# One list of 2833 steps replaced by another, in packed attention with a SwiGLU MLP

## The chip, the cores and the metric

The kernel runs on one core of one Trainium2 chip. The metric is the device time of one execution in microseconds (us). A trace of one profiled execution shows what each engine did: PE (TensorE, the matmuls), DVE (VectorE), ACT (ScalarE), POOL (GpSimd) and SP (SyncE, which here issues the transfers).

## The reference

```python
def _attn_ref(q, k, v, p):            # q, k, v: 8 x 8 x 576 x 64; p: 8 x 8 x 32 x 64
    scale = 1.0 / np.sqrt(q.shape[-1])
    def sm_attn(qq, kk, vv):
        s = scale * np.matmul(qq, kk.transpose(0, 1, 3, 2))
        s = s - np.max(s, axis=-1, keepdims=True)
        a = np.exp(s)
        a = a / (np.sum(a, axis=-1, keepdims=True) + 1e-09)
        return np.matmul(a, vv)
    p_packed = sm_attn(p, k, v)
    return sm_attn(q, p_packed, p_packed)

def _moe_ref(x, w_gate, w_val, w_out, rms_g):   # x: 4608 x 512; w: 512 x 1536 (twice), 1536 x 512
    rms = np.sqrt(np.mean(x * x, axis=-1, keepdims=True) + 1e-06)
    xn = x / rms * rms_g
    g = xn @ w_gate
    silu = g * (1.0 / (1.0 + np.exp(-g)))
    return silu * (xn @ w_val) @ w_out
```

The 8 heads' attention outputs, 64 wide each, stand side by side as the 512 features of a token. The three weight matrices arrive in double precision, as pairs of 32-bit words.

## The kernel before, in words

Attention over 32 packed keys per head comes first, then the norm and the MLP. Stage 1 lets the 32 packed vectors of a batch attend to its 576 keys (scores L747 and L756, softmax L778, values L887). The 4608 tokens are cut into 12 units of 384; units 1, 4, 7 and 10 span two batches, so their attention has twice as many small matmuls. For a unit: scores of the queries against the packed keys (L1231, L1238), softmax (L1252 to L1262 on DVE, L1257 on ACT), attention values (L1309, L1318), norm and transposition into aTu, the MLP's input (L1136 on ACT and L1138 on DVE for unit 0, a transposing transfer issued at L1396 later), 24 blocks of gate and value matmuls (L1439), SiLU and products (L1520, L1523, L1542, L1545), output matmuls (L1506), store (L1577, L1580).

In the first 60 us or so the weights are fetched and turned into single precision on the chip: ACT (L387, L396), POOL (L391) and DVE (L393, L398, L401, L403) share the pieces, PE sums their squares (L447, L454), packed weights are formed for the first batches (L1040), and each piece is split into a high half (L352, ACT) and a low half (L354, DVE), kept in `ring`, which L1439 reads. Stage 1 of a later batch goes through a_0x and a_1x: exponentials are split into 16-bit halves, transposed by a transfer (L856), added up on POOL (L861), and only then used by PE (L887).

All this is written as some 90 coroutines ("chains", among them keys, stage 1, queries, attention, packed weights, one for each weight piece, the MLP, the stores). `Plan.run` walks the table ORDER: each pair of base-64 digits is a chain's number, and that chain issues its next step on that step's engine. So ORDER alone sets the order within each engine's stream. Buffers (four PSUM banks pm_0x to pm_3x, the halves psa and psb, six large buffers big_0x to big_5x, two each of aTu, o and others) go to the steps in the same order, so a table also decides which buffer a step has and whose release it waits for. FILLS lists at which PE steps how many filler matmuls are put in: L1603, 128x256 on constants, whose result nobody reads.

Of the kernel before, what the change touches and what calls it, by code (L numbers as in the profile page):

```python
# [44 lines left out]
class Plan:  # L45
# [89 lines left out]
    "ATAwAYAyArAvAYAxAWATAsAWAvAyAXAZAPAxArAsArArArAYArATAZAsAYATArAzAZAsAZATAyAzAZAyAaA0AoAsA0AsATAsAaAzArAaA0ATAsAT"
    "AzA1A1A1AsA1AoAcAsA0ATAcA2ArAdACATACATA3AsACAdARAcA3A2AfA2A3AdATAfA3A2ARACATAeA4A4ACATA4ATATAeAQAQA5ARATATACA5AC"
    "ATATAeARATACATATATATARATACAQACAgAfACARAgAQARACATASARACAhAQARAQAhAQARACA4AAAAAAAAAAAAARASA5ARAgAAARAQATARARARAQA6"
    "ATATATATARAhATATARA5ARASAQATATARARAAATATATA6ATARARAAA6AAA6A7ARATATARAQASAAAAARA8ATAAA9ARARAAAAAAATA8ATATATATA9AT"
    "ARATATAAATAAATARA9A-ARA9ARATATA+AABAA+BAATATASA+AABAA+ARASAABBAABABCBBATATBDAABCASARASAABCBBBDBCATATARBEBBBEBDBE"
    "BFBEBDATAAATATBFAAASARBGBFAABGBFASAAATBGBIBGATBHBHBHBHBIARAAATATASARBKBIARATARBKASBIBLBKBKARACBMBLARATATACBMBMBM"  # L140
    "ARBLBNBLBNARACACACACATATATATBOATBJAQBNATBNATATATATATACAQBOAQACARARAQARARARARARBPAQBPBOARACBPACBPACACBJAAAAARAAAC"
    "ACAQACBOACACATA-ATATATATATATATATAAAAACAAAAATAAAQATAAATATATATATACATACAQAQAAAAAQAAACATACAAACACAABQATA7ATACACAQBRBR"
    "ACATATATATACAAACACASBQAAAAASATACAbAbBSAAARBSASBSACAbAABSARATATASATATATBTBTATBTARBTBVATATARBVAbAABWBUBWATATATATBV"
    "BWBVBXASAABXAAASAABXBWBYBXARBZATBYACAbBZATARBYBaBaATATATAbBZAABYBaBbBZATAABbASAbBbBaBcACASAABcATATARBbARAABdBeAb"
    "AbAABeBdBcBdBdATATAbATARARASAbBcARBfATBeAbARARBeAbARBfBgBfATAbATBUAAACBgACARAbBgBfBhATATBgBjAbBjATATATATBhAbACAR"
    "ATATATARASACACBhBjACARARBiAQAQATAbACBhAbATARBkAbAQBkBjATATARATATACBkARARARARARBkACAQBlASACACACACAbACATATAQARBiAC"
    "ACACAAACAbATATATATATAAATACAQAQAbATATATATATATAQAbAQAAAQAABlAQAQATAAAAACAAACAAASAbAbBmACACAbAAACACBnBnAAACATACATAT"
    "ACATAAATACACACBnAbACBmATAABnAbASBoBoBoARBoARACATATBpAABpASAbATATAABqARBqBrATATARBqBsACAbBqBrBsATATATARAAAbBsBrBs"
    "BrAbATBtBtAbARACBuBtAABuBtAAATATBvAbACATATAABvATATBuBvAbARAABuBwBvAABwBxAABwAbBxARAABxAbATBwARARATATARARAbByATAT"
    "BxARARAAByBzAbByAAARByATAbBzARATBzB0ARB0ATAbB0BzARARAAAAB0ATB1ATAbATB1ARB2AAB1AQB1AQAQAAB2AAARAbB2ARAQB2ATATAbAT"  # L150
    "ATARATATATATATAQATAQAQARAQATATAQAbAQARACATATAbARAQAbATATAbB4ACAbARAbATATATATATATAbATATACARARARAbACAbATATATATB4AT"
    "ATAbACATATATACAbB3B5AbACAbARARAbARAbACAbACACARACAbACB3B5AAAAAAAAATACAbATATATAAAAATB6AAAbACB7ATATB8ACARARB7ASAbB7"
    "AbB8ATB8B7B-AbB8B9B9B9B9AbATATATACB-ACARB+AbAAB-AAAAB+B-ASATB+CBCACACAB+AbCAATATCBAbARATATARARCCCCASCBAbARARACCB"
    "AAACCDCDAAAbARB6CCCEATCEATACCECDCECDAAACCCCFAAASCFATCFARARCFATCGCGCGACACCHATAACGAAACARATCHACARACARCIATCHAAATACCH"
    "ARARCIACACARCJARARATARAAATATAQACAAATCIARATAQCIATACCJCKACAAAAATATAQCJCJASAACLCKAQACARCKCKAQAAATATATATATCLACATATAQ"
    "CLAQAQATATATATATATATAQAQAAATATCLAQASAAAAAAAACMATATCOARCNACATATATARATARATATAACOCNACCNARATATARCPACCNACARACATATATAT"
    "ATATARCQCRATATCSCRCRCSACCRATATASCSARACACCTCUCTCUCUCTATATACCSCTACARCVCUARARATATCVASARCVCWCVARATARCXCWATACCXCYARCY"
    "CXCWACACACCYCWCXACASCZCZCZATATATAACaCZAAAACMACCYCaARATATATCbCaCbATARATCaCbCcACARACCcAACbCPACCdCcATCdATCcATATAQCQ"
    "AAAAAAARAQARACCeAQCdAACdAACeATCfATAQAAACATATATATARAAAACfARARATASACAQAACfCeACARARAQCgATCfACAQATAAAQATCeACCgAQARAA"
    "AQACACACATACATATATAAATATATAQATATATACATATACChCgACCgACACASAAAQAACiATATATATATAACiAACjARCiAAAAARCiAAARASATATATATCkAC"  # L160
    "ATATATATATATCjCkAACkATARAACkARClCmATATATCnAACmATATCnAACmAACnCnARCoCmCoATATCpCoCoATCqACCpACARAACpCqCqCpATATATCrAC"
    "CqACCrARACATATATCrCtCrCtACARATACATCtCuCuARACARCtCvARCuACCvARCvATATARCuATCwCvCwATATATAQClCxARAQAQARCsACACARCxCwAQ"
    "CwAQARAQAQCyCxATATATATCyATCyATACACACACCxATATCyARChARAAACATARARAQARAQATATAAACARATATATATATATATATAAARATATAAAAATATAT"
    "ATAQARARATATATATAAARAQAAAAARAAARATCzACAAAAAAAAARC0CsACACARATATATAAAAATATATACATATACCzC1AAAAARC2ARC2ATAAATATATC3C2"
    "C3ASC2C4C3C4ACC4C3ATATARC5ACAAC5C5C6C5C6ACC6ACASATACC7ARC6ATC7ACC7AAC8C7ACC8ATATATATC4ACC8C9AAACC9ACC8AAC-AAARAC"
    "C9ASC9C+C+C-ACC+ARC+ARATATDAACATC-DAAAC-ASATARDADCDAATACDBDBDBAAARDBARATDCDDAADCATATAADDAADDDCDEATARARATATDDATAT"
    "ATATAQDFARATACDEAQDFARC0DFARASACATATACARAQARARDEAADFATDHDEATATATARDGAQDGDHDGARARAQDIAQASACARAQARDJDGARATATATAQDJ"
    "ATATATATATATATATDHATAQACDHDHATACDJAQATATATATDIATATATDKDHDHARAQARATATATATATACDKDHDJARDHARACDLATATATDMDNARDMATATDN"
    "DMACDMACASDODNDPDODPDODPDPDNATATDOATATDQDQDRDQDHATATDRDQDSDRDHASDTDSDRDTATATATDTDTDUDSATATDSDUACARDVDVDUASDHDUAT"
    "DWACARDXACDXDWDXACDXDVACATATATDVDYDWDYDYATATDZDHDYDZATDaAQC1AQDHACDaATATARATATDLDZASARAQACATATAQACARARDaATARARDZ"  # L170
    "AQACARARDaDWAQARAQATATATATATDcATACATATAQAQDbACARAQAQARATATARARACARDbATATARAQACARDcARATARATACACACATACATATATATARAT"
    "ATATARACACACACACDbDdARACASATDeDdATDbARDeARASATATDfATATDfACDeDfACDeDfARATATACDgATATATARDhDiARDhDiATDhDiDhATDjDjDj"
    "ATATATDiDjDkATATDkDlARDlACDkARATATATDlDlDmDmDkDmDnDmATATDoATARDoDnATDoDoDnARARDnATDpATATARDpDpDqDpARDqATATDqATAQ"
    "DrDqDrAQAQAQAQAQAQDrARDsAQDsATATATATATDrARAQDsATATATARARAQARDsARATATATATATARATATATATARAQDgATATATARARARARARATATAT"
# [1478 lines left out]
```

## Time and profile before

| | |
|---|---|
| median of 3 runs | 736.81 us (735.4 to 737.38) |
| profiled execution | 735.02 us, of which the span takes 732.8 us |
| granted clock of TensorE over the span | 0.998 of full speed |
| PE busy | 712.7 us, 97% of the span |
| DVE, ACT, POOL busy | 468.9, 476.0, 210.2 us |
| PE idle from 0 to 60 us | 8.7 us (60 less 51.31 busy) |
| last 13 us | PE busy 9.31 us |

The span runs from the first instruction to the last; the profiled time has some 2.2 us around it. PE is the engine that nearly fills the span, so the table is read by where PE has nothing to do, and why: in the first 60 us, in a few waits later, and at the end while the last tile is stored.

### The profile page before, as it was taken

Reading aid. Unit: us, or ns where it says so; the run is one execution under the profiler, and the core shown is the slowest. Engines: PE = TensorE matmul, PEld = TensorE weight load, DVE = VectorE, ACT = ScalarE, POOL = GpSimd, SP = SyncE. Lnnn points to the kernel's source line nnn. Section 1 sums busy time; section 2 is a strip of 40 time slices with the busy share of each in tenths; the row PEclk is TensorE's granted clock in tenths of the full one; section 3 lists DMA queues with packets and bytes.
Section 4 is the critical chain, followed back from the end, with each engine's and each line's share of the span. In section 5 each row is a group of like instructions: output and inputs, shape, how many; then the busy total and the mean of one; then the engine's idle time right before and its main releaser. Section 6 shows DMA issues by size and latency. Waiting matters only on the chain.

```text
span 732.8 us, 19527 instructions
## 1 busy us (share of the span) xinstructions
PE 712.7 (97%) x8164; PEld 432.1 (59%) x8164; DVE 468.9 (64%) x1032; ACT 476.0 (65%) x982; POOL 210.2 (29%) x228
## 2 busy tenths in 40 slices
...
GB/s 288 369 376 266 203 3 65 85 155 198 34 145 116 145 91 142 169 89 118 81 195 79 65 180 109 102 101 133 73 115 57 62 67 80 65 3 50 1 1 58
DMA packets 152922, 86.72 MB, mean 118 GB/s; under 512 B 116737, under 2 KB 140161, under 8 KB 152834
## 3 DMA queue, kind: packets, MB, share of 16 engines
...
q14 instruction: 24, 0.20, 0.1%
...
## 4 chain that ended last, share of the span: by engine, by line
PE 83%; DMA 6%; ACT 4%; DVE 3%; issue 2%; SPq 1%; POOL 0%; ACTq 0%; DVEq 0%; POOLq 0%
PE pm_3x L1439 10%; PE pm_2x L1506 10%; PE pm_1x L1439 9%; PE pm_2x L1439 9%; PE pm_0x L1439 9%; PE pm_0x L1506 7%; PE pm_1x L1506 7%; PE pm_3x L1506 6%; DMA ring<-in_moe_w_val_dram 2%; PE psa L1238 1%; DMA a_1x<-hl_0x 1%; PE psb L887 1%; DMA a_0x<-hl_0x 1%; PE pm_0x L1464 1%; PE pm_3x L1464 1%
## 5 line engine op out<-in xcount | busy, mean ns | idle before, releaser
L1439 PEld LDWEIGHTS <-ring 128*128 128x128 f16 x2304 | 204.4, 98 | 85.6 <-issue 13.2
L1506 PEld LDWEIGHTS <-hall 128*128 128x128 f16 x1188 | 113.5, 98 | 137.9 <-issue 8.5
L1545 POOL TENSOR_TENSOR hall<-t_1x,hall 128x384 f16<-128x384 f32 x67 | 64.3, 960 | 204.7 <-ACT hall L1542 196.1
L1545 POOL TENSOR_TENSOR hall<-t_0x,hall 128x384 f16<-128x384 f32 x61 | 58.6, 961 | 155.2 <-ACT hall L1542 150.4
L1506 PE MATMUL pm_2x<-wo,hall 128*128 128x512 f16 x360 | 81.2, 379 | 0.0
L1506 PE MATMUL pm_1x<-wo,hall 128*128 128x512 f16 x324 | 72.6, 379 | 0.6 <-ACT t_1x L1520 0.6
L1506 PE MATMUL pm_0x<-wo,hall 128*128 128x512 f16 x324 | 72.6, 379 | 0.0
L1439 PE MATMUL pm_3x<-aTu_1x,ring 128*128 128x384 f16 (+1 forms) x318 | 46.9, 290 | 0.1
L1439 PE MATMUL pm_3x<-aTu_0x,ring 128*128 128x192 f16 (+1 forms) x330 | 44.7, 280 | 0.0
L1439 PE MATMUL pm_2x<-aTu_1x,ring 128*128 128x192 f16 (+1 forms) x330 | 43.5, 276 | 0.5 <-DVE o_0x L1577 0.5
L1542 ACT CAST hall<-t_1x 128x384 f16<-128x384 f32 x69 | 34.9, 506 | 12.5 <-DVE t_1x L1523 12.3
L1542 ACT CAST hall<-t_0x 128x384 f16<-128x384 f32 x70 | 35.5, 507 | 11.6 <-DVE t_0x L1523 11.2
L1439 PE MATMUL pm_1x<-aTu_0x,ring 128*128 128x384 f16 (+1 forms) x288 | 42.4, 290 | 0.1
L1506 PE MATMUL pm_3x<-wo,hall 128*128 128x512 f16 x180 | 42.4, 389 | 0.0
L1439 PE MATMUL pm_0x<-aTu_0x,ring 128*128 128x384 f16 (+1 forms) x276 | 40.0, 288 | 0.0
L1439 PE MATMUL pm_1x<-aTu_1x,ring 128*128 128x384 f16 (+1 forms) x252 | 37.9, 292 | 0.9 <-issue 0.9
L1439 PE MATMUL pm_2x<-aTu_0x,ring 128*128 128x384 f16 (+1 forms) x258 | 37.8, 289 | 0.1
L1439 PE MATMUL pm_0x<-aTu_1x,ring 128*128 128x384 f16 (+1 forms) x252 | 36.6, 288 | 0.0
L1074 POOL TENSOR_TENSOR wgv<-o_0x,wgv 128x512 f16<-128x512 f32 x16 | 19.0, 1188 | 24.6 <-ACT wgv L1072 24.6
L1520 ACT ACT_TABLE_LOAD x15 | 19.2, 1283 | 10.4 <-PE pm_0x L1439 4.5
L861 POOL TENSOR_TENSOR a1T_0x<-a_1x 96x768 f32<-96x768 f16 x5 | 8.2, 1633 | 33.4 <-DMA a_1x<-hl_0x 33.4
L352 ACT ACTIVATE ring<-pm_0x 128x512 f16<-128x512 f32 x17 | 10.1, 592 | 7.7 <-PE pm_1x L1052 6.2
...
## 6 DMA issues: line engine op xcount, KB each, us to landing
...
```

Of the source, the lines that this page charges most:

```text
L352: nc.scalar.activation(hi, x, AF.Copy, scale=s)
L861: nc.gpsimd.tensor_tensor(a1T, x[:, 0], x[:, 1], ALU.add)
L887: nc.tensor.matmul(pp[32 * j : 32 * j + 32, :D], a1T[:, c, 32 * j : 32 * j + 32], vf[:, j, cv, :], start=(c == 0), stop=(c == NCK - 1),)
L1074: nc.gpsimd.tensor_tensor(wgv16[:, c, k, 1], st, wgv16[:, c, k, 0], ALU.subtract)
L1238: nc.tensor.matmul(ps2[o : o + n, i, :, pi, :], qT[:, lq, i, pi, o : o + n], packs[b][3][:, lp, pi, :, :], start=(j == 0), stop=(j == 2),)
L1439: nc.tensor.matmul(psi[:, :, o : o + n], pw[:, g, lw, w, f * P : (f + 1) * P], aT[:, :, la, g, o : o + n], start=(j == 0), stop=(j == 5),)
L1464: nc.tensor.matmul(pos[i], hall[:, ft, lh, i * P : (i + 1) * P], wo[:, ft, 1 - lw, :], start=(ft + n3 == 0), stop=(ft == NFT - 1 and n3 == 2),
L1506: nc.tensor.matmul(po, hall[:, ft, lh, ts], wo[:, ft, 1 - lw, :], start=(n == 0), stop=(n == 3 * NFT - 1))
L1520: nc.scalar.activation(t, pss[0][:, :UT], AF.Silu, scale=sc[:, c, 0:1])
L1542: nc.scalar.copy(hall[:, ft, 0, :], t)
L1545: nc.gpsimd.tensor_tensor(hall[:, ft, 1, :], t, hall[:, ft, 0, :], ALU.subtract)
```

## The change

The strings of ORDER and the tuple FILLS are replaced by others. Both lists have 2833 steps, the same steps of the same chains; no instruction's form changes. FILLS goes from 110 filler matmuls to 99. Ahead of the first gate matmul (L1439) there are 98 fillers where there were 110, and 21 transpositions of keys on PE (L628) where there were 27; the other six stand behind it.

```diff
 ORDER = (
-    "AEAEAAAAAAAAADAAAAAAAEAAADAAAAAAAAAAAAAAAAAAAEADAAAAAAAQAFABABAGAHAIAJAiAQAiAiAjAQAiAjAQAiAiAFAFAiAiADAiAjADAQAj"
...
+    "AEAAAAADAEAAAAAAAAAAAAADAAAAAAAAAAAAAAAAAAADAAAAAAAiAjAEAiAjAQAQAiAiADAiAFAQABAFABAiAiAjAQAjADAEAiAiAjAjAjAQAjAG"
...
 FILLS = (
-    (0, 30, "pm", 0), (5, 4, "psc", 0), (8, 5, "pa", -1), (24, 11, "pm", 0), (25, 8, "pm", 2),
-    (27, 37, "pm", 0), (30, 13, "psc", 0), (42, 2, "psc", 0),
+    (0, 30, "pm", 0), (5, 4, "psc", 0), (8, 5, "pa", -1), (18, 4, "psc", 0), (23, 5, "psc", 0),
+    (25, 7, "pm", 0), (26, 8, "pm", 0), (28, 32, "pm", 0), (31, 3, "psc", 0), (54, 1, "psc", 0),
```

The first place is VectorE early in the weight conversion. `t24`, `e_0x` belong to the softmax of unit 0, `wo32_78` is a raw weight piece, `wgv_77` the converted one, `tiny_13x` the sum of squares of a piece. Before:

```order
L1254 TENSOR_TENSOR e_0x_108<-psa_100,t24_0x_244 128x768
L398 SCALAR_TENSOR_TENSOR wgv_77<-wgv_77,wo32_78 128x4x256
L452 TENSOR_REDUCE tiny_13x_153<-pm_1x_95 128x2
L1259 TENSOR_REDUCE t24_1x_245<-e_0x_108 128x24
L1260 TENSOR_SCALAR t24_2x_246<-t24_1x_245 128x24
L1261 RECIPROCAL t24_2x_246<-t24_2x_246 128x24
L1262 TENSOR_TENSOR e_0x_108<-e_0x_108,t24_2x_246 128x768
L398 SCALAR_TENSOR_TENSOR wgv_77<-wgv_77,wo32_78 128x4x256
```

After:

```order
L1254 TENSOR_TENSOR e_0x_108<-psa_100,t24_0x_244 128x768
L452 TENSOR_REDUCE tiny_13x_153<-pm_3x_97 128x2
L398 SCALAR_TENSOR_TENSOR wgv_77<-wgv_77,wo32_78 128x4x256
L340 TENSOR_SCALAR tiny_14x_154<-pm_3x_97 128x2
L344 TENSOR_SCALAR tiny_14x_154<-tiny_14x_154 128x2
L345 TENSOR_SCALAR gv_r_80<-tiny_14x_154 128x2
L460 TENSOR_SCALAR ratio_81<-tiny_14x_154,gv_r_80 128x1
L398 SCALAR_TENSOR_TENSOR wgv_77<-wgv_77,wo32_78 128x4x256
L1259 TENSOR_REDUCE t24_1x_245<-e_0x_108 128x24
L1260 TENSOR_SCALAR t24_2x_246<-t24_1x_245 128x24
L1261 RECIPROCAL t24_2x_246<-t24_2x_246 128x24
L1262 TENSOR_TENSOR e_0x_108<-e_0x_108,t24_2x_246 128x768
```

The softmax sums and the division (L1259 to L1262) move behind one conversion (L398), and a piece's sum of squares with the four small steps that form its scale (L452, L340 to L460) moves ahead of two. In PE's stream the first packed weights (L1040) stood right behind the 16 L447 matmuls of that piece; now eight fillers and the sum over partitions of the piece (L454) stand between.

The second place is VectorE at the end of that stage, where its half of aTu(0), the first MLP input, is written (L1138). Before:

```order
L1023 TENSOR_SCALAR pgh_0x_132<-pg_0x_128,ratio_81 128x128
L354 SCALAR_TENSOR_TENSOR ring_87<-pm_2x_96,gv_r_80,ring_87 128x512
L393 SCALAR_TENSOR_TENSOR wgv_77<-wgv_77,wo32_78 128x4x256 x2
L594 COPY pT_0x_122<-pm_2x_96 128x256
L354 SCALAR_TENSOR_TENSOR ring_87<-pm_1x_95,gv_r_80,ring_87 128x512
L1138 SCALAR_TENSOR_TENSOR aTu_0x_111<-psa_100,aTu_0x_111 128x3x256
L354 SCALAR_TENSOR_TENSOR ring_87<-pm_3x_97,gv_r_80,ring_87 128x512
```

After:

```order
L1023 TENSOR_SCALAR pgh_0x_132<-pg_0x_128,ratio_81 128x128
L393 SCALAR_TENSOR_TENSOR wgv_77<-wgv_77,wo32_78 128x4x256 x2
L1138 SCALAR_TENSOR_TENSOR aTu_0x_111<-psa_100,aTu_0x_111 128x3x256
L594 COPY pT_0x_122<-pm_2x_96 128x256
L354 SCALAR_TENSOR_TENSOR ring_87<-pm_1x_95,gv_r_80,ring_87 128x512
L354 SCALAR_TENSOR_TENSOR ring_87<-pm_0x_94,gv_r_80,ring_87 128x512
```

Two low halves of weight pieces (L354) and the copy of the packed vectors (L594) move from ahead of L1138 to behind it. On ACT, two high halves (L352) move from ahead of aTu(0)'s other part (L1136) to behind it, and one query copy (L1175) the other way.

The third place is SyncE's queue of transfers around the second transposition of stage 1 for batch 2 (L856 on `a1_1x`). Before:

```order
L573 DMA pf_0x_121<-in_p_dram 32x2x64 x2
L1396 DMA_TRANSPOSE aTu_0x_111<-hl_0x_109 128x12x128
L573 DMA pf_0x_121<-in_p_dram 32x2x64
L1580 DMA out_0_dram<-o_1x_116 128x512
L573 DMA pf_0x_121<-in_p_dram 32x2x64
L551 DMA big_3x_105<-in_k_dram 96x4x384
L856 DMA_TRANSPOSE a1_1x_118<-hl_0x_109 128x12x128
L551 DMA big_4x_106<-in_k_dram 96x4x384
```

After:

```order
L573 DMA pf_0x_121<-in_p_dram 32x2x64
L551 DMA big_3x_105<-in_v_dram 96x4x384
L573 DMA pf_0x_121<-in_p_dram 32x2x64 x3
L1396 DMA_TRANSPOSE aTu_0x_111<-hl_0x_109 128x12x128
L551 DMA big_4x_106<-in_k_dram 96x4x384
L856 DMA_TRANSPOSE a1_1x_118<-hl_0x_109 128x12x128
L551 DMA big_0x_102<-in_k_dram 96x4x384
```

A store (L1580) and two of the loads of packed vectors (L573) no longer stand between the transposition of aTu and this one; a load of keys (L551) still does, and another stands behind it. PE's stream between the scores of that half batch (L756) and the values that need the transposition (L887) holds 51 output matmuls L1506 in both kernels.

## Rows read from the trace of the kernel before

**Rows 1.** The page: the span's heading and the busy times.

```profile
span 732.8 us, 19527 instructions
...
PE 712.7 (97%) x8164; PEld 432.1 (59%) x8164; DVE 468.9 (64%) x1032; ACT 476.0 (65%) x982; POOL 210.2 (29%) x228
```

**Rows 2.** Busy time by stretch: us from the start, length, each engine's busy time (instructions), granted clock, DMA share, GB/s.

```profile
0.00:60.00 60.00, 51.31 (x749) 39.23 (x750) 44.72 (x98) 41.28 (x72) 18.95 (x38) 1.00 1.02 349
...
60.00:733.00 673.00, 661.43 (x7418) 392.88 (x7416) 424.15 (x934) 434.68 (x911) 191.23 (x191) 1.00 0.45 98
```

**Rows 3.** What PE waited for before 60 us: line and releaser, total us, times, longest.

```profile
PE pm_1x L1603 <- POOL misc L263: 1.7, 1, 1.7
PE psb L454 <- DVE tiny_19x L452: 1.5, 1, 1.5
```

**Rows 4.** What PE waited for from 60 us on, the three that cost most.

```profile
PE psb L887 <- POOL a1T_0x L861: 3.4, 2, 1.8
PE psa L1318 <- issue: 2.1, 1, 2.1
PE pm_1x L1439 <- issue: 0.9, 1, 0.9
```

**Rows 5.** PE in the first conversions: start, us, engine, line, operation.

```profile
30.55 0.40 PE L1040 MATMUL pm_3x<-wgv,pg_0x 64*32 64x256 f32 x1
...
31.57 4.21 PE L1603 MATMUL pm_0x<-misc,margin 128*128 128x256 bf16 x37
36.75 0.85 PE L1112 MATMUL psb<-ident,e_0x 128*128 128x128 f32 x6 [0.96 <-ACT ring L352]
```

**Rows 6.** VectorE from 31 to 37 us.

```profile
31.03 0.96 DVE L1254 TENSOR_TENSOR e_0x<-psa,t_0x 128x768 f32<-128x768 f32 x1
31.90 1.22 DVE L398 SCALAR_TENSOR_TENSOR wgv<-wgv,wo 128x1024 uint32<-128x1024 uint32 x1
33.03 0.68 DVE L452 TENSOR_REDUCE tiny_13x<-pm_1x 128x2 f32<-128x512 f32 x1
33.63 0.94 DVE L1259 TENSOR_REDUCE t_1x<-e_0x 128x24 f32<-128x768 f32 x1
...
35.16 1.44 DVE L1262 TENSOR_TENSOR e_0x<-e_0x,t_2x 128x768 f32<-128x768 f32 x1
```

**Rows 7.** ScalarE from 35 to 41 us.

```profile
35.95 0.70 ACT L352 ACTIVATE ring<-pm_3x,gv_r 128x512 f16<-128x512 f32 x1
...
39.94 0.58 ACT L1122 ACTIVATE aT_0x<-psb 128x512 f32<-128x512 f32 x1
```

**Rows 8.** VectorE's last instructions ahead of the first attention block aTu(0).

```profile
57.90 0.41 DVE L594 COPY pT_0x<-pm_2x 128x256 f32<-128x256 f32 x1
58.23 0.73 DVE L354 SCALAR_TENSOR_TENSOR ring<-pm_1x,gv_r,ring 128x512 f16<-128x512 f32 x1
58.89 0.94 DVE L1138 SCALAR_TENSOR_TENSOR aTu_0x<-psa,aTu_0x 128x768 f16<-128x768 f32 x1
```

**Rows 9.** PE around the first MLP matmuls.

```profile
60.00 0.49 PE L628 MATMUL pm_0x<-ident,big_1x 128*128 128x128 f32 x3
60.33 1.14 PE L1439 MATMUL pm_2x<-aTu_0x,ring 128*128 128x384 f16 x6
```

**Rows 10.** The chain that ended last, 150 to 185 us: start, us, what.

```profile
167.22 5.53 DMA a_1x<-hl_0x
...
176.82 5.42 PE pm_3x L1506 x18
```

**Rows 11.** The chain at 233 us, the same transposition of the next batch.

```profile
232.92 3.70 DMA a_1x<-hl_0x
```

**Rows 12.** The chain at 332 us, as many output matmuls.

```profile
331.81 3.88 PE pm_2x L1506 x18
```

**Rows 13.** Busy time by stretch, 176 to 182 us.

```profile
176.00:182.00 6.00, 6.00 (x26) 2.32 (x24) 2.96 (x11) 4.81 (x14) 0.00 (x0) 0.72 0.91 219
```

**Rows 14.** The chain at 435 us, inside the attention of unit 7.

```profile
434.89 2.14 issue
```

More of the change, by code (lines that the diff above doesn't have):

```diff
@@ L135 @@
[L135 to L174, printed above, removed]
@@ new lines @@
+    "AHAiAjAFAiAFAjAQACAjAQAGACACACACAHAHAFACAFACAGAFAIARAJAGACAFAKALASAIAIAHAHAJAJARAHAHASARAIAHAJAKARAkARASALAKAKAk"
+    "AMALAkALAkARANASAlAMARAJALAJAJAlAJARAlANANAQAQAHARARALAMAFALASAlARAMARALANASARARARASAmAOAPAUAmAAAAAAAQARAQAQAAAA"
+    "ANAQARASARAmANARAOAQAnANAmARAOAnAVAPAoAPARAQANALASARAOAPASARApAnAWAAAAAAAPApApAAApAUAUAUAAAoAPAJAVAVAnATATAtAVAT"
+    "AUAPATAuAtATAPAAAWAWAAAAAAAWAVAtAXATAAAuASAUAtAvATAWAuAYAXAAAuAvAVAAAAAAATAAAwAYAXAvAoAoArASAXAxAvAYArAwAqAZAxAT"
+    "ATAYAqAxAyArAyAwAxATATArAYArAZAyArAsAWAYANAsAZArAoArAXATArAyAwAZAXAsATArAPA0AsAZA0AoAzAZAaAzATAsA0ATAzA0AsAaAaA1"
@@ new lines @@
+    "AdAzA1A1AsATAsATATAdArAdAsA1ATAsA2AcA3A2AcACA2AeA2AsACATATACACA4A3ACAeACA3ARA4AcATACARACACACACATA3ATATAgATATA5AC"
+    "AeAQACARAQAQAfACAgAgATATA5ARASA5AAAQA5AAAAAAAhAAATATATAfATARATAQARARAQAQA4ARAfASARARATAQAAAhA6AQAQARA6ATARA6ATAR"
+    "ATARARARAAARAAAAA4ATATATATAhATARARARA6ATATASATARARAAASARAQA8AAAAA7ATARARA9AAA8AAARA9A8A8AAATATATATARARATATATAAAA"
+    "ARATAAATAAATATATATATARA-AAATATARA+ARAABAA+BAA+ASAAAAATBAA+A-ATASBBBBBABCBBARBCATATBDBBBCASARBCAABDARBDASBEBEBEAT"
+    "BEATBFATATAAATBFBDBGAABFAAASASBGATBGBFBIAABGBHBHBIAAARBHARARATATBKBHARARASBKBKARATASATBLBKARBMBIBLACATARBLBMACBI"
@@ new lines @@
+    "BLBMATBMATBNARBNATARARACATA7ATAQBJACACBOACBNACBNATAQATATACATATATBPATBOACARBPARARARAQARARBOACBPACBPBOACATATATATAA"
+    "ATBJAAAAACAAARAQACBQACACAAACACATAAATATATATATATAQAQACAQATAAAQAQAAAAAAAQATATATAAATACAAACATACAAACACACAAACATATATAQAT"
+    "ATACBRACACBRACASACBQASAAAAARAAAAAbACAbBSBSATAAASBSARATATASATATAbAAATBSAAARBTBTBTBUATBTARATATATBVACBWAABVBVAbBWAA"
+    "ARBVBWATATATATBWASBXBYBXAbBYBXARATATAABYBXBZAbASBaBYBZBZASBaARBZATATBbATATBbACAABaARAABbBcAbBaAABcARARBcAAAbBbAS"
+    "BdATATBcBeBdATATAbARBeARBfAbAbBeAbBeAABfAbATATATARBfBhBhAbBfARATBiBhACATATAbARACBiBhARAbAQAbBjACACACACAQARARARBi"
@@ new lines @@
+    "ATATATATBgATATBgBjBiATARAbATATAQAbAQACBjBdARBdAQASARARARARARAQBjAbACATATATATARATASACAQACBlAbACACACATATAQAbACATAb"
+    "AQATATACACATATATATATAAAABUACAAAAAbAQBkACAbACATATATAQATBkAQATAAAAAAAbAAASACAAATAbBmAbBlAAACBlAAAbACAAACACAbACATAS"
+    "ACATATATACBlACAAACACBnACAbBnACASBnBoAbARBnBoBoBmASBoATARACAbATBpATBpBpAbAAATBpARBqBrAABrACBrAbBrATATBsAbATATATBt"
+    "BsBtATBsAAAAAbATARBsBtBuAAARBuAAACBtBuARATATATBvBuAABvAABwBvAbACBwBvBqAAATATBxBwAbATATAABxBwBxARBxARARByARARByAT"
+    "ATARATATAbARBzByBzAbARARARBzATAAARByATB0AbAAARBzARB0B0B0B1ATATATAAATATATATATB1AAARAQB1B1B2AQAQAAARB2AbB2B2AQAAAR"
@@ new lines @@
+    "ARARARAQARAQAQARATATATATATATATAbAQACAbAQARATATATATATATATATAbARAQAbAbACB4AbAbACACACACAQAbAbATAbAbAbATATATARATATAT"
+    "ATATATATATATARB5ACB4ARACB3B3ARAbACAbACACACATATATATARAbACB5AbARB6ACAbAAAAAAAAB7ATAbAAAAATATAAAbAAB8AAB7B8AAARAAAC"
+    "B7B8AbATASB7B9B-B9B9AbB-B-ACB-AbB8ATATARAAB+ACB+B9AbASCAATCAATATARAbCAAbB+CBCAATATAbARCBCBB+CCAbCCCBAbARARASAAAC"
+    "CCATCECDARCDAbATARATACAbCCCDACAACECDASCECFACACCFCGARCEACAACGATATCHACATCGACARACCGATATAAACCFCHAACHCFATARCHCICIAAAA"
+    "ARACCJATATCICIATCJAACKCJARAAAACKAQACARAAAQATATATATCJARATATATATAAARARACAQACACARARAQACCKAQASB6AQATATARACAQAQARCKAT"
```

33 lines of the change are left out of this document (24 added, 9 removed).

## Prediction

> **What bounds the kernel now.** I read the page first: PE is busy for 712.7 us of a span of 732.8, the other engines for two thirds at most [rows 1]. So time goes down only where PE works less or waits less. The busy times by stretch tell where the 20.1 us of PE's idle time lie: 8.7 us in the first 60 us (60 less 51.31), 11.6 us in the 673 us behind (673 less 661.43; by 0.2 us more in sum, since the stretches end past the span) [rows 2]. The waits of PE tell for whom. Before 60 us the start itself takes 1.7 us, and the longest later one is 1.5 us for a VectorE reduction [rows 3]. From 60 us on there are 3.4 us in two waits for POOL's sum a1T_0x, and 2.1 and 0.9 us marked "issue", with no releaser that the profile shows [rows 4]. The wait of 1.8 us for POOL costs more than itself: in the stretch behind it the granted clock is 0.72 of full speed, so part of it ran at the lower level, 1.2 GHz, after PE had been idle [rows 13], and 18 output matmuls took 5.42 us there where 18 others took 3.88 [rows 10, 12]; 1.5 us more. The rest of the idle time is the last store, some 3.7 us, and short waits.
>
> **The fillers.** 110 go, 99 come. The 37 that stand in one row took 4.21 us [rows 5]; the last one alone shows 0.27, so one step is (4.21 - 0.27)/36 = 0.109 us, an estimate from that row. Eleven fewer are 1.2 us of PE's work. That is a gain only if PE isn't made to wait in their place, which the next part weighs. Behind 60 us no filler stands in either kernel, so the work there is the same apart from what moved across.
>
> **The start, up to the first gate matmul L1439.** It began at 60.33 us, straight behind the key transpositions (0.33 us for three, from their start to the next instruction's) [rows 9]. Ahead of it 12 fillers go (1.31 us) and six transpositions move behind it (0.66 us): PE would be there at 60.33 - 1.97 = 58.36 us if it waited as long as before. What it needs there is aTu(0), whose second part VectorE wrote from 58.89 to 59.83 us [rows 8]. In the new list VectorE has two low halves at 0.73 us and one copy at 0.41 us fewer ahead of it [rows 8], 1.87 us: ready at 57.96, and 0.5 us later, as before, the matmul can start: 58.46. ScalarE, two high halves fewer and one copy more ahead of its own part, loses nothing there. So by work alone the two sides come forward by the same amount, and 0.1 us of new waiting is left.
>
> **What speaks against it: three steps that come later.** First, the packed weights L1040 began at 30.55 us [rows 5]. Now the sum of squares of the second piece must be reduced first, behind the maximum subtraction that ended at 31.99 (31.03 + 0.96): 0.68 us of reduction gives 32.7, then L454 and L1040, some 2.2 us late. ScalarE read their first result only at 35.95 [rows 7], while the block ends at about 32.8 + 1.0 = 33.8 (it ended at 31.57, where the fillers start): covered, with 2.1 us to spare. Second, the softmax sums L1259 began at 33.63 and the division ended at 36.60 (35.16 + 1.44) [rows 6]. They now stand behind a second conversion L398, which before came right behind the division at 36.5; what it reads was ready on ScalarE one conversion, about 1 us, ahead of the 35.95 of [rows 7]: at about 35.0, an estimate. With 1.22 us that gives 36.2 for L1259, 2.6 us late. PE turns the quotient at 36.75 to 37.60 [rows 5], and ScalarE picked the result up only at 39.94 [rows 7]: 2.3 us of cover for 2.6 us, 0.3 us too few. Third, each low or high half that moved behind aTu(0) is needed by a later gate block of unit 0: three low halves in a row at 0.73 us against six matmuls at about 1 us a block (1.14 us with the last one's own length [rows 9]) keep pace. I take 0.1 + 0.3 and 0.2 for what is not seen, 0.6 us of new waiting, between bounds of -1.5 us (the longest VectorE wait of this stretch, gone [rows 3]) and +4.6 us (the second rival).
>
> **The middle and the end.** The work of PE between scores and values of the half batch that stalls is 51 output matmuls in both lists, so PE comes to the values as early as before. The transposition took 5.53 us there [rows 10], and 3.70 us at the next batch [rows 11]. A store and two small loads go from in front of it, a load of keys stays, another follows it as before. I take it as unchanged, 0, with -3.3 us (1.8 and 1.5) as the lower bound if the wait goes with its slow stretch, and +1.8 us as the upper one, a second wait of that size at a place that now just passes. At the end the order of units 10 and 11 is the same and so are the 3.7 us: 0.
>
> **The waits marked "issue".** They stand in the attention values of the two-batch units, inside a run of small matmuls: 2.14 us at 434.89 in the chain [rows 14]. PE's stream there has moved by a few instructions only and nothing is released in these waits, so I keep them: 0. The Trainium skill, "Runtime: NRT & Kernel Launch", section "Instruction fetch mechanics", says that an engine fetches its next block of instructions while it executes the current one and that this is mostly hidden. The rows don't say whether these waits are fetches. Read by that page nothing would wait there, and the sum would be 3.0 us lower; the trace has the 3.0 us, and I go by the trace.
>
> **The sum.** -1.2 (fillers) + 0.6 (start) + 0 + 0 = -0.6 us. The durations come from the profiled execution of 735.02 us, 1.8 us below the median of 736.81; the difference carries over: 734.4 for such an execution, and 736.2 for the median.
>
> **Rivals.** One, faster by the middle: the transposition for the half batch lands earlier, since fewer transfers stand ahead of it. At 4.0 us, near the 3.70 of the next batch, it is 1.5 us earlier, PE waits 0.3 us, and the slow stretch with its 1.5 us doesn't come: -3.0 - 0.6, 733.2 us. For it: the store and loads that moved. Against it: the load of keys right ahead of it, half a megabyte, is still there.
>
> Two, slower by the start: the late softmax decides. The reckoning above hides 2.6 us under 2.3 us of slack on ScalarE and trusts that VectorE, with less work ahead of aTu(0), catches up. If the chain from the division through transposition, values, norm and aTu(0) is bound by its own length, all 2.6 us arrive at the end: the first L1439 starts at 60.33 + 2.6 = 62.9 us, PE has been ready since 58.36, and that is 4.6 us of new waiting against 1.2 us saved: +3.4, 740.2 us. For it: VectorE worked 44.72 of the first 60 us, with most of its idle time before the conversions, so it has little room to catch up [rows 2]. Against it: aTu(0)'s last writers stood behind weight work, not behind their inputs [rows 8]. The point from which it decides: a first L1439 later than 61.8 us makes the kernel slower by 0.3%.
>
> Three, the two "issue" waits go: moved by a few instructions, the small matmuls may lie otherwise to whatever holds PE there. -3.0 - 0.6, 733.2 us. For it: only some of these units wait though all have the same matmuls. Against it: their places in the stream hardly move.
>
> Four, the new list doesn't do what it is said to: what it was judged by isn't what this trace shows, and the moves cancel out, waits taking the place of the fillers one for one: 736.8 us. It can't be told from the forecast by its time.
>
> **Chances and range.** About 0.3%, 2.2 us, is what a measurement of this kernel can tell from no change. The forecast and the fourth rival, both within it, have 0.48 together (0.40 and 0.08); the first rival 0.22 and the third 0.06, both faster; the second 0.20, slower; 0.04 is left for what I don't see, half to each side. That is 0.30 faster, 0.48 same, 0.22 slower. The likeliest case's own range is -1.2 - 1.5 to -1.2 + 1.8 + 0.6, 734.1 to 738.0. The range for 8 in 10 takes in most of the first and third rivals and the second up to near its price: 732.3 to 740.0 us.
>
> **What would show it right or wrong.** Right: the first L1439 at 58.4 to 59.2 us, PE idle for 9.0 to 9.6 us up to 60 us or for as long in the same work, two waits for a1T_0x of 1.5 to 1.8 us and one slow stretch near 170 us, and about 3 us of "issue". The late steps are shown by L1040 at 32.5 to 33.3 us and L1259 at about 36.2. Wrong: a first L1439 behind 61.8 us; more than 12 us of PE idle time before 60 us; a wait for a1T_0x under 0.5 us or a third one; or a new wait in the middle that the list brings about by another buffer being handed to a step.

## The result and the profile after

The changed kernel took 728.66 us (median of 4 runs, 728.2 to 731.87) against 737.10 (735.4 to 738.89): ratio 0.9895, 95% interval 0.9858 to 0.9931. With six more runs beside 20 of before the ratio was 0.9899 (0.9875 to 0.9924). The gain is some 8 us. The forecast was 736.2, between 732.3 and 740.0: the time lies 7.5 us below the forecast and 3.6 us below the range. The profiled execution took 728.67 us, 6.35 less than the one of before.

The head of the page of the changed kernel, to be held against [rows 1]:

```profile
span 726.8 us, 19520 instructions
...
PE 708.9 (98%) x8153; PEld 431.8 (59%) x8153; DVE 465.2 (64%) x1032; ACT 476.5 (66%) x982; POOL 213.4 (29%) x228
```

PE's busy time fell by 3.8 us, and its idle time from 20.1 to 17.9 us. Busy time by stretch, against [rows 2] (the second stretch again runs past the span, by 0.2 us):

```profile
0.00:60.00 60.00, 50.58 (x741) 38.48 (x742) 45.13 (x99) 42.06 (x73) 23.22 (x39) 1.00 1.02 348
60.00:727.00 667.00, 658.34 (x7414) 393.36 (x7412) 420.10 (x934) 434.42 (x910) 190.21 (x189) 1.00 0.45 99
```

Up to 60 us PE is idle for 9.4 us where it was 8.7; nearly all of the gain comes later. The waits of PE from 60 us on, against [rows 4]:

```profile
PE psb L887 <- POOL a1T_0x L861: 2.7, 2, 1.4
PE pm_1x L1506 <- issue: 0.7, 1, 0.7
PE pm_0x L1439 <- issue: 0.7, 1, 0.7
```

The waits marked "issue" fell from 3.0 us to 1.4, and the two for POOL from 3.4 to 2.7. One of these two has moved: it stands no longer ahead of the second half batch, behind the 5.53 us of [rows 10], but ahead of the first, as the chain that ended last shows. In the kernel before, that chain had

```profile
154.55 3.99 DMA a_0x<-hl_0x
...
174.59 0.88 PE psb L887 x48
```

and in the changed kernel it has

```profile
154.07 5.49 DMA a_0x<-hl_0x
...
161.31 0.88 PE psb L887 x48
```

No stretch of half clock follows. Where the stretch from 176 to 182 us had a granted clock of 0.72 [rows 13], it has 1.00 now:

```profile
176.00:182.00 6.00, 6.00 (x89) 3.20 (x88) 4.15 (x16) 5.54 (x16) 0.00 (x0) 1.00 0.69 186
```

At the same output matmul behind both kernels' start, the one that waits 0.59 us for ScalarE, the traces stand at 155.68 and 155.19 us, before and after:

```profile
155.68 1.67 PE L1506 MATMUL pm_1x<-wo,hall 128*128 128x512 f16 x7 [0.59 <-ACT t_1x L1520]
155.19 2.10 PE L1506 MATMUL pm_1x<-wo,hall 128*128 128x512 f16 x9 [0.59 <-ACT t_1x L1520]
```

That is 0.5 us for start and fillers. The difference of the spans, 6.0 us, is then 0.5 (start and fillers), 1.5 (the slow stretch, [rows 10, 12]), 0.7 (POOL), 1.7 (issue) and 0.5 (a wait of L1439 for the copy ahead of a store, L1577, gone): 4.9. The other 1.1 us are spread over shorter pieces that I can't assign.

Two traces are two executions. Each run also reports its span and its mean granted clock, and those tell what slow stretches do to the time. All runs of before (67 in all the comparisons below) had a mean clock of 0.9973, the changed kernel's 10 runs one of 0.9976: slow stretches, in which the granted clock is well below 1, come about as often in either. In runs with a mean clock of 1.000, with none of them in the body, the span was 732.0 us in the mean for before (11 runs) and 725.7 for the changed kernel (3 runs: 724.9, 725.3, 726.8). So 6.3 us are gained at full clock, and another 0.4 lies outside the span (2.2 us before, 1.8 after). The slow stretch of the first trace explains next to nothing of the mean.

### The profile page after: what moved, and what is told of

Read it like the earlier page. It is cut to its first block, busy times and chain, and to the rows that moved or that the text cites. A ratio compares the mean times of both kernels' runs of the same rounds, so it can differ in the third digit from the quotient of the medians.

```text
span 726.8 us, 19520 instructions
## 1 busy us (share of the span) xinstructions
PE 708.9 (98%) x8153; PEld 431.8 (59%) x8153; DVE 465.2 (64%) x1032; ACT 476.5 (66%) x982; POOL 213.4 (29%) x228
## 4 chain that ended last, share of the span: by engine, by line
PE 83%; ACT 5%; DMA 4%; SPq 3%; DVE 2%; issue 1%; POOL 1%; ACTq 0%; POOLq 0%; DVEq 0%
PE pm_2x L1439 10%; PE pm_0x L1506 10%; PE pm_1x L1439 9%; PE pm_3x L1439 9%; PE pm_1x L1506 9%; PE pm_3x L1506 9%; PE pm_0x L1439 8%; PE pm_2x L1506 5%; DMA hall<-in_moe_w_val_dram 2%; SPq L423 2%; PE psa L1238 2%; PE psb L887 1%; PE pm_1x L1052 1%; PE psa L756 1%; PE pm_0x L1052 1%
## 5 line engine op out<-in xcount | busy, mean ns | idle before, releaser
L1439 PEld LDWEIGHTS <-ring 128*128 128x128 f16 x2304 | 205.1, 98 | 83.8 <-issue 10.7
L1506 PEld LDWEIGHTS <-hall 128*128 128x128 f16 x1188 | 113.3, 98 | 137.1 <-issue 6.7
L1506 PE MATMUL pm_1x<-wo,hall 128*128 128x512 f16 x360 | 80.8, 379 | 1.3 <-issue 0.7
L1506 PE MATMUL pm_3x<-wo,hall 128*128 128x512 f16 x324 | 73.2, 379 | 0.0
L1506 PE MATMUL pm_0x<-wo,hall 128*128 128x512 f16 x324 | 72.6, 379 | 0.0
L1439 PE MATMUL pm_2x<-aTu_0x,ring 128*128 128x384 f16 (+1 forms) x318 | 45.7, 287 | 0.0
L1439 PE MATMUL pm_1x<-aTu_1x,ring 128*128 128x192 f16 (+1 forms) x318 | 44.7, 284 | 0.0
L1439 PE MATMUL pm_2x<-aTu_1x,ring 128*128 128x192 f16 (+1 forms) x324 | 44.7, 282 | 0.0
L1439 PE MATMUL pm_3x<-aTu_0x,ring 128*128 128x192 f16 (+1 forms) x306 | 42.4, 282 | 0.0
L1506 PE MATMUL pm_2x<-wo,hall 128*128 128x512 f16 x180 | 40.0, 379 | 0.0
L1439 PE MATMUL pm_3x<-aTu_1x,ring 128*128 128x192 f16 (+1 forms) x270 | 38.9, 287 | 0.2 <-ACT t_1x L1520 0.2
L1439 PE MATMUL pm_1x<-aTu_0x,ring 128*128 128x384 f16 (+1 forms) x246 | 38.8, 299 | 0.1
L1439 PE MATMUL pm_0x<-aTu_0x,ring 128*128 128x192 f16 (+1 forms) x282 | 38.0, 279 | 0.7 <-issue 0.7
L1439 PE MATMUL pm_0x<-aTu_1x,ring 128*128 128x384 f16 (+1 forms) x240 | 36.5, 294 | 0.0
L1074 POOL TENSOR_TENSOR wgv<-o_1x,wgv 128x512 f16<-128x512 f32 x20 | 23.4, 1172 | 41.3 <-ACT wgv L1072 41.1
L1520 ACT ACTIVATE t_0x<-pm_0x,usc_1x 128x384 f32<-128x384 f32 x13 | 7.5, 577 | 22.3 <-PE pm_0x L1439 21.6
L354 DVE SCALAR_TENSOR_TENSOR ring<-pm_1x,ring 128x512 f16<-128x512 f32 x17 | 11.7, 685 | 14.7 <-ACT ring L352 14.6
```

The costliest lines, as they stand in the source:

```text
L354: nc.vector.scalar_tensor_tensor(lo, x, s, hi, ALU.mult, ALU.subtract)
L1074: nc.gpsimd.tensor_tensor(wgv16[:, c, k, 1], st, wgv16[:, c, k, 0], ALU.subtract)
L1439: nc.tensor.matmul(psi[:, :, o : o + n], pw[:, g, lw, w, f * P : (f + 1) * P], aT[:, :, la, g, o : o + n], start=(j == 0), stop=(j == 5),)
L1506: nc.tensor.matmul(po, hall[:, ft, lh, ts], wo[:, ft, 1 - lw, :], start=(n == 0), stop=(n == 3 * NFT - 1))
L1520: nc.scalar.activation(t, pss[0][:, :UT], AF.Silu, scale=sc[:, c, 0:1])
```

## The experiments

"Old" is the list of before, "new" the changed one. Medians are of device time; "before" is the kernel before in the same round of runs; "mean clock" is the mean over a kernel's runs of the granted clock; a dash in the last column means that no run had a mean clock of 1.000.

| kernel | median, us | before | ratio (95% interval) | mean clock | mean span at clock 1.000 |
|---|---|---|---|---|---|
| before_again | 736.09 (one run) | 736.02 | | 0.998 | - |
| new_head_old_rest | 731.81 | 736.02 | 0.9955 (0.9933 to 0.9978) | 0.9974 | 728.2 |
| old_head_new_rest | 734.03 | 736.02 | 0.9977 (0.9961 to 0.9992) | 0.9989 | 731.8 |
| new_start_old_rest | 741.81 | 736.02 | 1.0087 (1.0059 to 1.0114) | 0.9925 | - |
| new_again | 727.70 | 735.86 | 0.9899 (0.9875 to 0.9924) | 0.9978 | 725.1 |
| old_99_fillers | 735.56 | 735.86 | 0.9998 (0.9979 to 1.0018) | 0.9966 | - |
| old_filled_waits | 730.08 | 735.86 | 0.9929 (0.9909 to 0.9949) | 0.9987 | 728.0 |
| new_filled_waits | 728.94 | 735.86 | 0.9917 (0.9891 to 0.9943) | 0.9984 | 725.5 |
| new_110_fillers | 734.17 | 736.65 | 0.9971 (0.9943 to 1.0000) | 0.9958 | 728.5 |
| old_shift_only | 732.61 | 736.65 | 0.9948 (0.9930 to 0.9966) | 0.9993 | 730.2 |
| old_fill_no_shift | 738.00 | 736.65 | 1.0026 (1.0006 to 1.0046) | 0.9935 | - |
| new_filled_start | 728.97 | 736.65 | 0.9898 (0.9879 to 0.9917) | 0.9978 | - |

**Before once more.** No edit.

> The kernel before, unchanged, profiled once more. Theory A (the difference lies in fixed places of the list): the same waits in the same places, an execution of 735 to 736 us with one wait of about 1.8 us ahead of L887 near 173 us, a slow stretch behind it, and 2.1 and 0.9 us of issue near 435 and 267 us. Theory B (the profiled execution of before was a lucky one): more slow stretches or longer issue waits than in the first trace, 737 us or more, at other places.

The waits of PE from 60 us on, and the stretch behind the longest of them:

```profile
PE psb L887 <- POOL a1T_0x L861: 2.8, 2, 1.4
PE psa L1318 <- issue: 2.2, 1, 2.2
PE pm_1x L1439 <- issue: 1.3, 1, 1.3
```

```profile
436.00:440.00 4.00, 3.58 (x17) 1.84 (x18) 0.00 (x0) 2.54 (x9) 2.31 (x3) 0.61 0.75 173
```

The same waits stand in the same places, the issue waits at 2.2 and 1.3 us. The slow stretch has moved: the clock is 1.00 behind the wait for POOL at 175 us (1.4 us here, 1.8 in the first trace), and 0.61 of full speed behind the 2.2 us of issue. So the waits belong to the list, and a slow stretch follows one or another of them from run to run.

**Old and new spliced.** After 725 steps both lists have issued the same set, so they can be cut there (179 us). The edits of the three spliced kernels are written here as expressions; the kernels hold the strings that come of them.

```diff
-ORDER, FILLS = OLD, FILLS_OLD
+ORDER, FILLS = NEW[:725] + OLD[725:], FILLS_NEW
```

> The new list for its first 725 steps, up to the output matmuls at 179 us, then the old list; at this cut both lists have issued the same set of steps, so nothing else changes. Theory A1 (the gain comes from the slow stretch and the waits up to 179 us): three tenths of the gain shown by the traces at this place, 2.5 us, and the issue waits of the old list stay: about 734.5 against 737. Theory A2 (the gain lies behind 179 us): no difference beyond 0.6 us, the share of the fillers and the start. Theory B: the gain depends on how often slow stretches come, and most of the 8 us may show here.

Measured: 4.2 us less in the median, more than the traces had shown for this part. The trace fell on the slowest of its runs, with a wait of 1.5 us ahead of L454 in the start, a slow stretch behind it, and 4.58 us for 24 matmuls L1231; the first L1439 came at 62.72 us, and another wait of 3.2 us, for ScalarE (L844), stands at 82 us:

```profile
27.02 4.58 PE L1231 MATMUL psa<-misc,big_2x 128*128 128x64 f32 x24
```

But the issue wait at 267 us, which both traces of before show, was gone, and the one near 435 us was down to 1.2 us (put down to a product on VectorE), though the list of that part was the old one. That spoke against A1 and A2 alike: a part that wasn't changed had lost its waits. Eleven fillers fewer ahead had moved its place in PE's stream by 22 instructions.

```diff
-ORDER, FILLS = OLD, FILLS_OLD
+ORDER, FILLS = OLD[:725] + NEW[725:], FILLS_OLD
```

> The other way round: the old list up to step 725 (179 us), then the new list. Theory A1: the gain of the rest alone, 3.5 us by the traces (issue waits 0.8 and 1.4 us, drift later 0.9), about 733.5. Theory A2: nearly the whole gain, 729 to 730. Theory B: under 2 us of gain.

Measured: 2.0 us less, and at full clock only 0.2. The new rest alone gains next to nothing, because with the old head in front it has longer issue waits than in the changed kernel:

```profile
PE pm_0x L1052 <- issue: 1.4, 1, 1.4
PE pm_1x L1439 <- issue: 1.0, 1, 1.0
...
PE pm_3x L1439 <- issue: 0.3, 1, 0.3
PE psa L1318 <- issue: 0.3, 1, 0.3
```

These are 3.0 us, where the changed kernel had 1.4 in its first trace. The changed kernel gains 1.0%, head and rest by themselves 0.45 and 0.23%: the issue waits depend on both.

**The start alone.** The first 400 steps of the new list, then what is left in the old order.

```diff
-ORDER, FILLS = OLD, FILLS_OLD
+ORDER, FILLS = NEW[:400] + [s for s in OLD if s not in NEW[:400]], FILLS_NEW
```

> The new list for its first 400 steps only (the weight conversions, the first attention, unit 0 up to about 100 us) and the new fillers, then the steps that are left in the order of the old list. The prediction's sum for the start and the fillers: -0.6 us, so no difference that can be measured. If the start is what matters more than the traces say: -2 us or more.

Measured: 5.8 us slower; both expectations failed. The splice, where the sets weren't equal, brought a wait of its own, 4.5 us at 108 us for a softmax division that now comes late on VectorE:

```profile
107.03 0.97 DVE e_0x L1262
...
108.14 1.52 PE psb L1112 x6
```

So it tells nothing of the start, and is left aside.

**The changed kernel once more.** No edit.

> The changed kernel, unchanged, with more runs beside the kernel before and one more profile. Theory A (the gain is of fixed size): a median of 728 to 730 us against 736, ratio 0.989 to 0.992, and the same waits as in its first trace. Theory B (the first runs were lucky, slow stretches come in most of them): 731 us or more.

Theory A held in the main: 727.7 us, 0.3 below its range, at a ratio inside it. The waits are not all the same: the one for POOL at 161 us is missing, and the issue wait at 433 us is 0.3 instead of 0.7 us. The trace fell on the slowest run (731.15), with a slow stretch in the start, and the first L1439 came at 62.7 us instead of 58.8.

```profile
31.00:35.00 4.00, 4.00 (x29) 3.38 (x29) 2.42 (x3) 3.44 (x4) 0.00 (x0) 0.50 1.05 389
```

**Fewer fillers in the old list.**

```diff
-    (27, 37, "pm", 0), (30, 13, "psc", 0), (42, 2, "psc", 0),
+    (27, 26, "pm", 0), (30, 13, "psc", 0), (42, 2, "psc", 0),
```

> The old list with 11 fillers fewer (26 instead of 37 in the longest row), so 22 instructions fewer in PE's stream behind them, as in the new list. If only the fillers' time counts: 0 to -1.2 us. Theory S (the issue waits hang on where the stream stands): the wait of 0.9 to 1.3 us at 267 us, which all three kernels with the old list's start showed and none with the new one's, goes, and the 2.1 to 2.2 us near 435 us get shorter: -1 to -3 us altogether. Rival (the issue waits hang on the order of the steps or on the transfers): they stay as in the old list.

Measured: no difference. In the trace the wait at 267 us is gone and at the place of the other stands one of 1.1 instead of 2.1 us (put down to VectorE), as theory S said, but the time was spent elsewhere: a slow stretch at 38 us, soon behind the shortened row (mean clock over the runs 0.9966, and none of the 12 had 1.000), and a transposition that took 6.49 us, for which PE waited 2.75 us.

```profile
38.00:42.00 4.00, 4.00 (x32) 3.49 (x32) 3.90 (x9) 3.45 (x5) 0.77 (x1) 0.57 1.05 383
```

```profile
168.59 6.49 DMA a_1x<-hl_0x
...
176.93 0.88 PE psb L887 x48
```

At equal clock a gain shows: five runs at 0.998 have a mean span of 731.3, and 25 runs of before at 0.998 one of 733.6. Of these 2.3 us the fillers' own work can be 1.2.

**The waits for POOL filled.** 12 fillers each ahead of the two L887 steps.

```diff
+    (199, 12, "psc", 0), (278, 12, "psc", 0),
```

> The old list with 12 more fillers (1.3 us) just ahead of each of the two L887 steps that wait 1.4 to 1.8 us for POOL's sum, near 173 and 237 us. Theory C (the slow stretch behind the first of these waits comes from PE standing idle): no slow stretch there in the trace, the waits shorten to 0.1 to 0.5 us, and the time falls by 0.5 to 1.5 us, the price of the stretch times how often it comes. Rival (the stretch comes anyway, or the fillers delay L887): the time is the same or up to 2.6 us longer. The stream behind is 24 and 48 instructions longer, so the issue waits may change too.

Measured: 5.8 us less, four times the most that theory C allowed for, with the old list and 24 instructions that compute nothing. All waits of PE from 60 us on:

```profile
PE pm_1x L1506 <- ACT t_1x L1520: 0.6, 1, 0.6
PE pm_2x L1439 <- DVE o_0x L1577: 0.5, 1, 0.5
PE pm_2x L628 <- DVE pT_0x L594: 0.3, 1, 0.3
PE psb L499 <- DVE wo_ss L502: 0.2, 1, 0.2
```

The waits for POOL are gone, as filled, but so is every issue wait; filling and shifting had been done at once. The next kernels separate them.

```diff
-    (23, 5, "psc", 0),
+    (23, 17, "psc", 0), (180, 12, "psc", 0), (279, 12, "psc", 0),
```

> The new list with 12 more fillers ahead of the L454 that waits 1.5 us at 27 us, and ahead of the two L887 steps that wait 1.3 to 1.4 us (near 161 and 236 us). Theory C: slow stretches at these places go; in the trace with the new start and the old rest one came at 27 us (24 matmuls L1231 took 4.4 us instead of 2.9). The spread of the runs narrows, and the median falls by 0 to 1.5 us against the new list. Rival: the fillers delay what follows, up to 1.3 us each, and the median rises by 1 to 4 us.

Measured: 1.2 us above the changed kernel's median of 727.70, within the noise of both (intervals 0.9891 to 0.9943 and 0.9875 to 0.9924). At full clock the spans are the same (725.5 and 725.7). The new list has little left there to win, and the spread of the runs (727.0 to 735.1) did not narrow.

**Shift without filling.** 24 fillers where PE waits for nothing, at 195.7 us in the trace of before.

```diff
+    (225, 24, "psc", 0),
```

> The old list with 24 more fillers at 195.7 us, in the middle of gate matmuls where PE waits for nothing: they cost 24 x 0.109 = 2.6 us of work and shift the stream behind by 48 instructions, as the filled waits did. Theory S: the issue waits at 267 us (0.9 to 1.3) and 435 us (2.1 to 2.2) go from the trace, and the time is 0.5 to 1 us below that of the kernel before in spite of the 2.6 us. Rival (the filled waits helped by filling, not by shifting): both issue waits stay and the time is 2.6 us longer, 738.5.

Measured: 4.0 us less than before, with 2.6 us of work more. All waits from 60 us on:

```profile
PE psb L887 <- POOL a1T_0x L861: 1.8, 2, 1.1
PE psb L499 <- DVE wo_ss L502: 1.1, 1, 1.1
PE pm_1x L1506 <- ACT t_1x L1520: 0.6, 1, 0.6
PE pm_2x L1439 <- DVE o_0x L1577: 0.5, 1, 0.5
```

The waits for POOL are still there, 1.8 us in all; no issue wait is. Theory S had allowed for a gain of 0.5 to 1 us. At full clock the span is 730.2, and 727.6 without the 2.6 us of fillers: 4.4 us below the 732.0 of before. The two issue waits of before, 3.1 and 3.5 us in its two traces, are most of that. Not all of it is the shift: the fillers also hold PE back by 2.6 us ahead of the second wait for POOL, which is 0.8 us here and was 1.4 to 1.6.

**Filling without shift.** Both waits filled, and 24 fillers fewer in the start.

```diff
-    (27, 37, "pm", 0), (30, 13, "psc", 0), (42, 2, "psc", 0),
+    (27, 13, "pm", 0), (30, 13, "psc", 0), (42, 2, "psc", 0),
+    (199, 12, "psc", 0), (278, 12, "psc", 0),
```

> The old list with its two L887 waits filled by 12 fillers each and 24 fillers fewer in the longest row of the start (13 instead of 37), so that the stream behind 237 us stands where the old one stands. Theory S: the issue waits near 267 and 435 us are back at 0.9 to 1.3 and 2.1 to 2.2 us, and most of the gain of the filled waits (5.5 us) is gone: 734 to 736, more if the shorter row lets a slow stretch in at 37 us. Rival (filling is what helped): 730 to 731.

Measured: 1.4 us slower than before. The longest waits from 60 us on:

```profile
PE psa L1318 <- issue: 2.1, 1, 2.1
PE pm_2x L1439 <- ACT a1T_0x L844: 1.5, 1, 1.5
PE pm_1x L1439 <- issue: 1.2, 1, 1.2
```

No wait for POOL is left, and the issue waits are back with the sizes of before, 2.1 and 1.2 us, since the stream stands where it stood. The gain of the filled waits is gone, and the time is 2 us above the range of theory S, which allowed for more if a slow stretch came; the mean clock is 0.9935. Slow stretches alone don't explain the loss: at a clock of 0.995 the spans are 734.3 to 735.2 us, and the run with filled waits and the shift at 0.995 had 729.0, with 24 fillers more.

**The new list shifted back.**

```diff
-    (25, 7, "pm", 0), (26, 8, "pm", 0), (28, 32, "pm", 0),
+    (25, 7, "pm", 0), (26, 8, "pm", 0), (28, 43, "pm", 0),
```

> The new list with 11 more fillers in its longest row (43 instead of 32), so that PE's stream stands 22 instructions later behind them, where the old list's stands. The issue waits stood at fixed numbers of PE's stream in the traces so far (7984 in eight, 3932 and 4443 in some). Theory S (they hang on where the stream's blocks end in the order of the steps): the waits of the trace with the old head and the new rest come back, 1.4 us near 248 and 1.0 us near 268 us, and the time rises by 2 to 3.5 us against the new list, to about 730. Rival (fillers cost their time and no more): 0 to 1.2 us.

Measured: 734.17, 5.5 to 6.5 us above the changed kernel and more than theory S gave. The number of fillers is that of the old list, and the stream stands where the old one's did. All waits from 60 us on, and the stretch behind the first:

```profile
PE pm_0x L1052 <- issue: 2.0, 1, 2.0
PE psb L887 <- POOL a1T_0x L861: 1.6, 2, 1.3
PE pm_1x L1439 <- issue: 1.0, 1, 1.0
PE pm_1x L1506 <- ACT t_1x L1520: 0.6, 1, 0.6
PE psa L1318 <- issue: 0.5, 1, 0.5
PE pm_2x L1439 <- issue: 0.3, 1, 0.3
```

```profile
246.00:250.00 4.00, 3.59 (x16) 1.37 (x16) 2.44 (x4) 2.72 (x5) 0.00 (x0) 0.59 0.02 5
```

The issue waits of the old head with the new rest have come back, 3.8 us in all, and one of them pulls a slow stretch behind it (clock 0.59; mean over the runs 0.9958). At full clock the span is 728.5: 2.8 us above the changed kernel, of which fillers can be 1.2 at most. The rest of the 5.5 to 6.5 us goes with the lower mean clock.

**A version meant to beat both.** 30 fillers in waits of the new list's start.

```diff
-    (18, 4, "psc", 0), (23, 5, "psc", 0),
+    (18, 14, "psc", 0), (23, 17, "psc", 0), (46, 8, "psc", 0),
```

> The new list with 30 more fillers, all inside waits of the start: 10 ahead of the second L887 (waits 1.3 us for a load at 21 us), 12 ahead of the first L454 (1.5 us at 27 us), 8 ahead of an L447 (0.9 us at 57 us). Theory C (slow stretches follow PE's idle time): fewer of them in the start, a mean clock nearer to 1 than 0.9978, 0.5 to 1.5 us off the median. Theory S: the stream stands 60 instructions later, so the issue waits change by up to 2 us either way. Rival: the fillers delay the start, +1 to +3 us.

All waits from 60 us on:

```profile
PE psb L887 <- POOL a1T_0x L861: 0.7, 1, 0.7
PE pm_1x L1506 <- ACT t_1x L1520: 0.6, 1, 0.6
PE pm_2x L1439 <- DVE ring L354: 0.3, 1, 0.3
PE psa L1318 <- issue: 0.3, 1, 0.3
```

It has as little issue wait as the new list with filled waits (0.3 us), and less wait for POOL, but it pays for that in the start: the output matmul that stood at 155.19 us stands at 157.72 in its trace. The median is 728.97, no better than the changed kernel (727.70 and 728.66). Its runs all stay between 727.8 and 730.3; the mean clock is the same, 0.9978, so theory C failed here.

## Why the prediction was wrong

**The step that failed is the one on the waits marked "issue":** "PE's stream there has moved by a few instructions only and nothing is released in these waits, so I keep them: 0." Added up before rounding, they were 3.1 and 3.5 us in the two traces of before and are 1.3 and 1.6 in the two of the changed kernel (0.6 of it put down to ScalarE). So the term was -1.7 to -2.0 us, the largest that the traces show beside the slow stretch. The move by a few instructions is what decides. (One of the two waits of before stands on a gate matmul, L1439, behind a run of L1318 and not inside one [rows 4].)

Number PE's records of a trace in order: matmuls, weight loads and semaphore steps. (Most f32 matmuls of the program are there as two matmuls with two loads.) From 60 us on the fourteen traces have 23 waits of 0.25 us or more marked "issue", and each stands 194 or 195 records past a multiple of 256, whatever stands there: at 6082 or 6083 in four traces, on L1052 or L1506; at 6594 or 6595 in six, on L1439; at 10434 or 10435 in ten, on L1318 in some and on L1439 in others; and at 14274 or 14275, short ones, in seven. These are 27 places, since in four cases the row names another engine, which came last there.

What ends these waits is in the traces too. Every run's DMA rows show a queue with 64 packets, of 16 KB each, one for each 256 of PE's 16347 to 16420 records, and the trace has each packet's start and length:

```profile
q8 instruction: 64, 1.05, 0.6%
```

In all 27 cases PE went on 1.1 to 1.5 us after the end of that block's packet (the 40th packet for 40 times 256, and so on). At the 848 other crossings that could be read, PE came there 1.4 us or more after it. In the trace of before the 40th packet ran from 434.44 to 435.74 us, and PE stood from 434.89 to 437.03 [rows 14]. In the old list shifted by 48 the 40th packet ended at 433.79, PE came to the crossing at 435.28, and there is no wait. So PE waits there for instructions that arrive late. The place is fixed, and the list decides which instruction is there and how soon PE gets there: in the old list the wait is longest, 2.1 to 2.2 us, inside the run of small matmuls L1318 of unit 7 [rows 14]. The shift by 48 at a place without waits took these waits out of the old list, the shift by 22 brought them into the new one, and filled waits without a shift left them standing.

The Trainium skill, "Runtime: NRT & Kernel Launch", section "Instruction fetch mechanics", says that each engine fetches its stream in blocks of 256 instructions while it executes, and that the cost of crossing into the next is mostly hidden. The packets of 16 KB and the waits at one place in each 256 agree with the blocks. That it is mostly hidden agrees for 848 of 875 crossings, and the runs differ on the rest: up to 2.2 us at one place, 3.8 us in one trace. Why one run of small matmuls comes too soon for its packet and another does not is not worked out here. The third rival had these waits in view, with 0.06, and held against itself that their places in the stream hardly move; a shift by 22 was enough, though not all of its 3.0 us came.

**Fillers:** -1.2 was the right price of the work, and the wrong reckoning. Taking 11 away in the old list alone gained nothing measurable, since slow stretches and a late transposition took what the shift gave. Up to 155 us, fillers and start together are worth 0.5 us between the traces, which is the -0.6 of the sum.

**The start:** right in its places. L1040 began at 32.94 us (forecast 32.5 to 33.3), the softmax sums at 35.74 (about 36.2), the first L1439 at 58.79 (58.4 to 59.2), and PE's idle time up to 60 us was 9.4 us (9.0 to 9.6):

```profile
32.94 0.40 PE L1040 MATMUL pm_1x<-wgv,pg_0x 64*32 64x256 f32 x1
```

```profile
35.74 0.94 DVE L1259 TENSOR_REDUCE t_1x<-e_0x 128x24 f32<-128x768 f32 x1
```

```profile
58.79 1.14 PE L1439 MATMUL pm_1x<-aTu_0x,ring 128*128 128x384 f16 x6
```

The second rival, the late softmax, didn't come to pass. What the forecast didn't have is that another execution of the same kernel reached that L1439 at 62.7 us, behind the 61.8 that it gave as a sign of being wrong, and was still some 5 us faster than before (731.15): the good agreement of the first trace is in part luck.

**The middle:** the wait moved. The forecast kept it ahead of the second half batch, from its load of keys; the transposition of the first half, which took 5.49 us here and 3.99 before, was not weighed. In size it is -0.7 us in the first trace, small as said. The signs named for it did not come: the two waits for a1T_0x are 1.4 and 1.3 us and not 1.5 to 1.8, there is no slow stretch near 170 us, and the issue waits are 1.4 us and not about 3.

**The slow stretch:** I took one that a single trace happened to show as part of the list. At 1.5 us it was well priced, but by the mean clocks such stretches come in both kernels about equally often.

**The profile as a base:** the sum was made against one execution at clock 0.998, and the forecast's own range left no room for a cause that no term stood for. The term of the issue waits was set to 0 with no bound on either side. It is the step that is shown to have failed; it isn't the whole of the difference.

What stays open: 6.3 us were gained at full clock. The first traces, with the slow stretch of 1.5 us taken off, differ by 4.5 us, of which 1.7 are issue waits, 0.7 POOL, 0.5 the copy, 0.5 start and fillers, and 1.1 not assigned. The other 1.8 us is how far these two executions lie from the means at full clock (731.3 against 732.0, and 726.8 against 725.7). So some 3 us of the 6.3 remain that no experiment isolates, and their cause is open.
